# A block of sliding attention and a gated MLP: PSUM tiles with one reader each, another order of the rest products, and another order in three slots

## The chip, the core and the metric

The kernel runs on one core of one Trainium2 chip. The metric is the device time of one execution in microseconds. The engines named below are TensorE (PE, with its weight loads PEld), VectorE (DVE), ScalarE (ACT), GpSimd (POOL) and SyncE (SP); SP and POOL mostly issue transfers. TensorE writes its results to PSUM, and VectorE or ScalarE copy them from there to SBUF.

## The reference

Two branches share a layer norm of x (2048 rows, 576 columns). Branch A is attention: 32 query heads over 16 key and value heads, the last 512 positions of the caches, no mask. Branch B is a gated MLP. The result is x + A * silu(B).

```python
def _A_ref(x, k_cache, v_cache, wq, wo):
    q = (x @ wq).reshape(B, Sq, Hq, Dh).transpose(0, 2, 1, 3)
    k = repeat(k_cache[:, :, Sk - W:, :], rep, axis=1)      # W = 512, rep = 2
    v = repeat(v_cache[:, :, Sk - W:, :], rep, axis=1)
    p = softmax(einsum("bhqd,bhkd->bhqk", q, k) * Dh ** -0.5)
    o = einsum("bhqk,bhkd->bhqd", p, v)
    return o.transpose(0, 2, 1, 3).reshape(B, Sq, Hq * Dh) @ wo

x = A_x
xn = layernorm(x)
s = _A_ref(xn, A_k_cache, A_v_cache, A_wq, A_wo)
g = silu(_B_ref(xn, B_w1, B_w2, B_w3, B_w4))
return x + s * g
```

## The kernel before

Attention is cut into 4 blocks of 512 query rows with 32 heads each, 128 units that the code counts with `u`. One pass of the loop at line 738 is called a slot here. In slot u TensorE makes the query product of unit u + 1 (`stage_q`), the scores of unit u in two halves (`stage_s`, called `scores(0)` and `scores(1)`), and the value product of unit u - 1 in two halves (`stage_v`, called `values(0)` and `values(2)`). Into some slots further work is laid: the output projection with wo of the block before (`wo_part(0)` to `wo_part(3)`, slots `wo_slots`: 45 to 49, 65 to 69 and 97 to 101) and layer-norm steps (`fill`).

The order on TensorE, SP and POOL is the order in which the code is written. VectorE's and ScalarE's order in the loop is the planner's, with the copies out of PSUM at high priority. In the startup ahead of the loop (lines 691 to 722) the order of all engines is as written.

**The query product.** x has 576 columns: four chunks of 128 and a rest of 64. For the first four heads the rest is padded and multiplied like a chunk (line 539). From head 4 on the rests of four or six heads are made together, in a run (`BURSTS`, 23 runs; 16 of six heads, and 7 of four). The rest products use 64 rows of the array each, and two of them go side by side. They are made in the slot ahead of the run's first head, by `rest_q(u, first)` at line 511: the rest of head u goes into the PSUM bank `psq` that already holds its four main products, that of head u + 1 opens the next `psq` bank, and those of the heads behind go in pairs into a tile of two banks each, borrowed from the scores. `score_bank(1)` (tag sc1) takes the second pair and `score_bank(0)` (tag sc0) the third. A pair is copied to SBUF (`rq`) at once, and `stage_q` adds it later, when it copies that head's main product to `qT` (line 547). For heads without `rq` line 549 copies `psq` to `qT`.

The second pair is copied by ScalarE (line 528). Of the third pair, VectorE copies one half and ScalarE the other (lines 525 and 526). Where a tile is read by two engines, the framework makes the second reader wait for the first.

Each half of the scores takes a tile of two banks, sc0 or sc1; ScalarE's exponential (line 560) empties it. In the wo slots both halves go to sc0 and the output projection takes sc1; it ends in a ScalarE copy (`so`, line 279 or 291). The value product has two banks (tag po), one for each half; VectorE empties them with a reciprocal and a product (lines 583 and 584).

**The order within a slot.** In a slot with a run ahead of it (`late_q`), `scores(0)` comes ahead of `stage_q(u + 1)`, and both halves of the values come ahead of `scores(1)`. Three slots are both of this kind and wo slots: 49, 69 and 101, each the last of its five. There the wo work is the narrow part of the projection, 128 products of 64 columns, in four equal parts (`cuts`, line 741).

**The startup.** x of the first block is transposed by TensorE into two PSUM tiles of two banks each (`x_banks`, line 457): four chunks in the first, the rest chunk in the second, which also takes the transposes of the first two key heads (`k01`). `xT_first` (line 467) copies chunks 0, 1 and 4 with VectorE and chunks 2 and 3 with ScalarE. Then come the query products of heads 0 and 1 (line 717). Later a table load for the exponential and the copies of the keys follow.

Of the kernel before, what the change touches and what calls it, by code (L numbers as in the profile page):

```python
# [8 lines left out]
P = 128  # L9
ACT = mybir.ActivationFunctionType  # L10
# [21 lines left out]
def kernel(  # L32
# [266 lines left out]
    with ExitStack() as actx:  # L299
# [155 lines left out]
            nc.sync.dma_start(out=dstT[:, :, tt * P:(tt + 1) * P], in_=src[:, tt, :], transpose=True)  # L455

        def x_banks():
            four = [ps_sc.tile([P, 4, QB], BF16, name="ps_x", tag=f"sc{i}") for i in range(2)]
            return [four[kc // 4][:, kc % 4, :] for kc in range(NDC)], four[1][:, 2:4, :]

        def tr1_first(pss, tts):
            for tt in tts:
# [45 lines left out]
            cols = slice(u % 4 * Dh, (u % 4 + 1) * Dh)  # L508
            return wq_b[(u // 4) % NWQ][:, kc, cols] if kc < NF else wr_first[:, cols]

        def rest_q(u, first):
            xT = xT_b[u // Hq % 2]
            psq_t[u + 1] = ps_pq.tile([P, QB], FP32, name="psq", tag="pq")
            n = bursts[u]
            pair = [score_bank(i) for i in ((0,) if u - 1 in wo_slots else (1, 0)[0:n // 2 - 1])]
            pss = [first, psq_t[u + 1]] + [p[:, i, :] for p in pair for i in range(2)]
            for i, ps in enumerate(pss):
                half = slice(i % 2 * DR, (i % 2 + 1) * DR)
                nc.tensor.matmul(ps[:, :], lhsT=wr_sb[half, (u + i) % Hq // 2, :], rhs=xT[half, NF, :],  # L519
                                 start=(i > 0), stop=(i != 1), skip_group_check=True)  # L520
            for k, p in enumerate(pair):
                rq = rq_pool.tile([P, 2, QB], FP32, name="rq")
                with tc.high_priority(offset=HP):
                    if k:
                        nc.vector.tensor_copy(out=rq[:, 0, :], in_=p[:, 0, :])
                        nc.scalar.activation(out=rq[:, 1, :], in_=p[:, 1, :], func=ACT.Copy)
                    else:
                        nc.scalar.activation(out=rq[:], in_=p[:], func=ACT.Copy)
                for i in range(2):
                    rq_t[u + 2 + 2 * k + i] = rq[:, i, :]  # L530

        def stage_q(u):
            qb = u // Hq
            plain = u < PLAIN
            pos = 0 if plain else u - first_of[u]
            psq = psq_t.pop(u) if pos == 1 else ps_pq.tile([P, QB], FP32, name="psq", tag="pq")
            n = NDC if plain else NF
            for kc in range(n):
                nc.tensor.matmul(psq[:, :], lhsT=wq_main(u, kc), rhs=xT_b[qb % 2][:, kc, :],  # L539
                                 start=(kc == 0 and pos != 1), stop=(kc == n - 1 and (plain or pos != 0)),  # L540
                                 skip_group_check=True)
            if not plain and pos == 0:
                rest_q(u, psq)
            qT = qT_pool.tile([P, QB], BF16, name="qT")
            with tc.high_priority(offset=HP):
                if pos >= 2:
                    behind["qT"] = nc.vector.tensor_tensor(out=qT[:, :], in0=psq[:, :], in1=rq_t.pop(u), op=ALU.add)  # L547
                else:
                    nc.vector.tensor_copy(out=qT[:, :], in_=psq[:, :])  # L549
            qT_t[u] = qT  # L550
# [186 lines left out]
        with tc.manual_schedule(engines={SP, POOL, PE}):  # L737
            for u in range(0, max(max(fill), max(pe_fill)) + 1):
                atoms = pe_fill.get(u, [])
                n = len(atoms)  # L740
                cuts = [0, n // 4, n // 2, 3 * n // 4, n]
                if u == U:
                    cuts = [0, n // 2, n // 2, 3 * n // 4, n]

                def wo_part(i):
                    for fn in atoms[cuts[i]:cuts[i + 1]]:
                        fn()

                def scores(i):
                    if u < U:  # L750
                        stage_s(u, i)

                def values(t0):
                    if 0 <= u - 1 < U:
                        stage_v(u - 1, t0)

                if u == 1:
                    stage_q(2)
                late_q = u + 1 in bursts
                if late_q:  # L760
                    scores(0)
                    if u in wo_slots:
                        wo_part(0)
                if 1 < u < U - 1:
                    stage_q(u + 1)
                if not late_q:
                    scores(0)
                for fn in fill.get(u, []):
                    fn()
                if not (late_q and u in wo_slots):  # L770
                    wo_part(0)
                values(0)
                wo_part(1)
                if late_q:
                    values(2)
                    wo_part(2)
                    scores(1)
                else:
                    scores(1)
                    wo_part(2)  # L780
                    values(2)
                wo_part(3)
                for fn in turn.get(u, []):
                    fn()
# [648 lines left out]
```

## Time and profile before

| what | value |
| --- | --- |
| median of 3 runs | 820.67 us (820.44 to 821.25) |
| the profiled execution's own time | 820.41 us |
| its span, first to last instruction | 818.9 us |
| granted TensorE clock | 1.000 |
| attention | up to about 470 us |
| first part of the MLP | about 479 to 530 us |
| the two large MLP products | about 530 to 815 us |

A line of the timeline has the start in us, the time until the end of its last instruction in us, the engine, the line of the kernel, the operation, the written tile, the read tiles, the shape, the number of instructions that were merged, and in brackets the idle time of the engine ahead of it with what ended it. A line of the waits names who waited for whom, the total in us, how often, and the longest. In a list of one tile or line, an instruction's durations stand as least, median and greatest in ns, with the first and last start in us.

### The profile page before, as it was taken

How to read it: one execution, taken by the hardware profiler on the slowest of the kernel's cores; microseconds unless marked ns; L12 is line 12 of the kernel's file. 1: busy time of each engine (PE TensorE's matmuls, PEld its weight loads, DVE VectorE, ACT ScalarE, POOL GpSimd, SP SyncE). 2: the span in 40 equal slices, each digit the busy share in tenths (PEclk: the TensorE clock that was granted, in tenths of full speed). 3: DMA queues.
4: the chain of work that ended last, by engine and by line, in shares of the span. 5: the costliest groups of instructions: out<-in, count | busy, mean ns of one | idle time of the engine just before them, and what ended most of it. 6: DMA issues, size and time to landing. Idle time of an engine off the chain costs nothing.

```text
span 818.9 us, 19757 instructions
## 1 busy us (share of the span) xinstructions
PE 805.9 (98%) x8158; PEld 471.3 (58%) x8239; DVE 458.5 (56%) x1395; ACT 412.2 (50%) x519; POOL 95.4 (12%) x162
## 2 busy tenths in 40 slices
PE   8999999999999999999999999999999999999997
PEld 6666565556655666555666556555555555555555
DVE  5879685128832579632676528443246636655413
ACT  6777776237733677822777542033233323334520
POOL 3333210100001000000100311272000000000000
PEclk9999999999999999999999999999999999999999
DMA  7995994109722656410553572399100410330101
GB/s 202 189 174 152 197 195 97 55 1 170 154 60 66 125 105 135 99 46 14 115 113 94 82 96 64 76 321 218 63 2 16 85 51 16 48 88 16 45 15 39
DMA packets 136430, 79.75 MB, mean 97 GB/s; under 512 B 113776, under 2 KB 127376, under 8 KB 136336
## 3 DMA queue, kind: packets, MB, share of 16 engines
q1 hardware_dynamic: 123792, 39.91, 27.7%
q0 software_dynamic: 11296, 37.27, 17.2%
q8 instruction: 65, 1.06, 0.6%
q10 hardware_dynamic: 1248, 1.25, 0.5%
q14 instruction: 29, 0.24, 0.1%
HBM read 45.38 MB, written 6.93 MB: 64 GB/s over the span
## 4 chain that ended last, share of the span: by engine, by line
PE 93%; DVE 4%; ACT 1%; issue 1%; POOL 0%; DVEq 0%; ACTq 0%; POOLq 0%
PE ph L1066 14%; PE po L579 13%; PE sc L557 12%; PE psq L539 12%; PE sc L269 12%; PE pm L1103 11%; PE pm L1281 4%; PE pm L1066 3%; PE pm L823 2%; PE pswo L269 2%; PE pr L1103 2%; PE ph L823 1%; PE pr L269 1%; PE sc L519 1%; PE pm L269 1%
## 5 line engine op out<-in xcount | busy, mean ns | idle before, releaser
L560 ACT ACTIVATE pT<-sc 128x1024 bf16<-128x1024 f32 x256 | 250.2, 1022 | 114.8 <-PE sc L557 106.6
L579 PEld LDWEIGHTS <-pT 128*128 128x128 bf16 x2048 | 133.4, 98 | 57.9 <-issue 6.4
L579 PE MATMUL po<-v_sb,pT 128*128 128x129 bf16 x2048 | 156.0, 220 | 0.7 <-ACT pT L560 0.4
L557 PE MATMUL sc<-qT,kT 128*128 128x512 bf16 x507 | 151.0, 379 | 0.4
L1066 PE MATMUL ph<-xT_b,w_s 64*128 64x512 bf16 x976 | 127.3, 376 | 0.0
L539 PE MATMUL psq<-xT_b,wq_b 128*128 128x512 bf16 x450 | 122.4, 379 | 2.8
L1103 PE MATMUL pm<-w_s,h 64*128 64x512 bf16 x864 | 122.1, 377 | 0.0
L1084 ACT ACTIVATE h<-ph 128x512 bf16<-128x512 f32 x67 | 39.4, 597 | 132.7 <-PE ph L1066 130.5
L269 PE MATMUL sc<-wo_sb,oT 128*128 128x512 bf16 (+1 forms) x756 | 101.8, 284 | 1.6 <-ACT so L279 0.8
L1103 PEld LDWEIGHTS <-h 64*128 64x128 bf16 x1728 | 70.6, 94 | 55.4
L269 PEld LDWEIGHTS <-oT 128*128 128x128 bf16 x1024 | 65.2, 98 | 56.3 <-issue 1.6
L584 DVE TENSOR_TENSOR o<-po,ri_b 128x256 bf16<-128x256 f32 x216 | 91.2, 422 | 6.3 <-DVE ri_b L583 0.3
L583 DVE RECIPROCAL ri_b<-po 128x2 f32<-128x2 f32 x256 | 42.4, 165 | 91.9 <-PE po L579 88.3
L1103 PE MATMUL pr<-w_s,h 64*128 64x64 bf16 x864 | 89.9, 189 | 0.0
L1066 PEld LDWEIGHTS <-w_s 64*128 64x128 bf16 x1152 | 55.8, 94 | 48.6 <-issue 0.6
L1082 DVE COPY hx<-ph 128x512 f32<-128x512 f32 x55 | 38.0, 691 | 60.6 <-PE ph L1066 60.6
L547 DVE TENSOR_TENSOR qT<-psq,rq 128x512 bf16<-128x512 f32 x78 | 53.9, 691 | 32.3 <-PE psq L539 31.7
L539 PEld LDWEIGHTS <-wq_b 128*128 128x128 bf16 x504 | 45.9, 98 | 41.6
L557 PEld LDWEIGHTS <-kT 128*128 128x128 bf16 x512 | 45.2, 98 | 29.7 <-issue 1.3
L549 DVE CAST qT<-psq 128x512 bf16<-128x512 f32 x48 | 33.0, 688 | 41.6 <-PE psq L519 25.9
L347 POOL DMA_DIRECT2D wq_b<-in_A_wq_dram x30 | 22.5, 752 | 279.4 <-PE psq L539 278.6
L1084 ACT ACTIVATE h<-hx 128x512 bf16<-128x512 f32 x55 | 34.6, 630 | 6.0 <-DVE hx L1082 1.7
(177 smaller groups left out, 697.9 us busy)
## 6 DMA issues: line engine op xcount, KB each, us to landing
wq_b<-in_A_wq_dram POOLq DMA_DIRECT2D x30, 512.0 KB, 5.0
wo_sb<-in_A_wo_dram POOLq DMA_DIRECT2D x8, 576.0 KB, 5.5
w_s<-in_B_w_dram POOLq DMA_DIRECT2D x9, 512.0 KB, 6.5
w_s<-in_B_w_dram POOLq DMA_DIRECT2D x10, 288.0 KB, 5.2
w_s<-in_B_w_dram POOLq DMA_DIRECT2D x4, 576.0 KB, 5.9
s_b<-s_dram SPq DMA_DIRECT2D x4, 576.0 KB, 6.6
x_b<-in_A_x_dram SPq DMA_DIRECT2D x4, 576.0 KB, 7.4
out_dram<-o SPq DMA_DIRECT2D x15, 144.0 KB, 1.8
```

The costliest lines, as they stand in the source:

```text
L269: nc.tensor.matmul(ps, lhsT=oT_t[qb * Hq + h][:, tt, :], rhs=wo_sb[:, h, lo:hi], start=(i == 0), stop=(i == Hq - 1))
L539: nc.tensor.matmul(psq[:, :], lhsT=wq_main(u, kc), rhs=xT_b[qb % 2][:, kc, :], start=(kc == 0 and pos != 1), stop=(kc == n - 1 and (plain ...
L547: behind["qT"] = nc.vector.tensor_tensor(out=qT[:, :], in0=psq[:, :], in1=rq_t.pop(u), op=ALU.add)
L557: nc.tensor.matmul(sc[:, j, :], lhsT=kT[:, g, kc * P:(kc + 1) * P], rhs=qT_t[u][:, :], start=True, stop=True)
L560: nc.scalar.activation(out=pT[:], in_=sc[:], func=ACT.Exp, scale=SCALE)
L579: nc.tensor.matmul(po[:, j, :], lhsT=pTs[kc][:, tt * P:(tt + 1) * P], rhs=v_sb[:, g, kc, 0:Dh + 1], start=(kc == 0), stop=(kc == KCH - 1))
L583: nc.vector.reciprocal(out=ri, in_=po[:, :, Dh])
L584: nc.vector.tensor_tensor(out=o[:, t0:t0 + 2, :], in0=po[:, :, 0:Dh], in1=ri.unsqueeze(2).to_broadcast([P, 2, Dh]), op=ALU.mult)
L1066: nc.tensor.matmul(ps[i][:, :], lhsT=lhsT, rhs=xT[half, kc, :], start=first, stop=last, skip_group_check=True)
L1082: nc.vector.tensor_copy(out=src[:, :], in_=ps[i][:, :])
L1084: nc.scalar.activation(out=h3[:, :], in_=src[:, :], func=ACT.Gelu_apprx_tanh)
L1103: nc.tensor.matmul(out, lhsT=h3_t[b, fc][half, tt * P:(tt + 1) * P], rhs=w4_s[fc // WS][half, fc % WS, lo:hi], start=key not in started, s ...
```

## The change

Five edits, all of them in attention and its startup.

1. `x_banks` takes three tiles instead of two. The first holds chunks 0 and 1 and the first two key heads (all read by VectorE), the second chunks 2 and 3 (read by ScalarE), and the third, borrowed from the values' po banks, chunk 4 (read by VectorE).
2. The third rest pair is copied by VectorE in one instruction of 1024 columns.
3. The rest products of a run are made in the order 2, 3, 0, 1, 4, 5.
4. `stage_q` is cut in two: `main_q` makes the four main products, `stage_q` the rest and the copy to `qT`. In slots 49, 69 and 101 `main_q` of the next head comes ahead of `scores(0)`. Everywhere else the order of these steps stays.
5. In the same three slots the wo work is cut otherwise: half of it behind `scores(0)`, none between the halves of the values, and a quarter each on both sides of `scores(1)`.

```diff
         def x_banks():
-            four = [ps_sc.tile([P, 4, QB], BF16, name="ps_x", tag=f"sc{i}") for i in range(2)]
-            return [four[kc // 4][:, kc % 4, :] for kc in range(NDC)], four[1][:, 2:4, :]
+            a, b = (ps_sc.tile([P, 4, QB], BF16, name="ps_x", tag=f"sc{i}") for i in range(2))
+            c = ps_po.tile([P, 2, W], BF16, name="ps_x4", tag="po")
+            return [a[:, 0, :], a[:, 1, :], b[:, 0, :], b[:, 1, :], c[:, 0, :]], a[:, 2:4, :]
...
-        def rest_q(u, first):
+        def rest_q(u):
+            first = psq_t[u]
...
-            for i, ps in enumerate(pss):
+            for i in (2, 3, 0, 1, *range(4, n)):
+                ps = pss[i]
...
                     if k:
-                        nc.vector.tensor_copy(out=rq[:, 0, :], in_=p[:, 0, :])
-                        nc.scalar.activation(out=rq[:, 1, :], in_=p[:, 1, :], func=ACT.Copy)
+                        nc.vector.tensor_copy(out=rq[:], in_=p[:])
...
-        def stage_q(u):
+        def main_q(u):
...
-            if not plain and pos == 0:
-                rest_q(u, psq)
+            psq_t[u] = psq
+
+        def stage_q(u):
+            if u not in psq_t or (u in first_of and first_of[u] == u - 1):
+                main_q(u)
+            pos = 0 if u < PLAIN else u - first_of[u]
+            if u in bursts:
+                rest_q(u)
+            psq = psq_t.pop(u)
...
-                if u == U:
+                if u == U or u + 1 in bursts:
                     cuts = [0, n // 2, n // 2, 3 * n // 4, n]
...
                 if late_q:
+                    if u in wo_slots:
+                        main_q(u + 1)
                     scores(0)
                     if u in wo_slots:
                         wo_part(0)
```

In the changed kernel the order of the instructions on SP and POOL is as before. On VectorE, in a run of six, both reciprocals of the values stand behind the long copy and both products behind them, and some layer-norm steps around a run come a few places earlier or later.

## The prediction

> **What bounds the kernel now.** I read the page first: busy shares, granted clock and the chain that ended last.
>
> ```profile
> span 818.9 us, 19757 instructions
> PE 805.9 (98%) x8158; PEld 471.3 (58%) x8239; DVE 458.5 (56%) x1395; ACT 412.2 (50%) x519; POOL 95.4 (12%) x162
> PEclk9999999999999999999999999999999999999999
> PE 93%; DVE 4%; ACT 1%; issue 1%; POOL 0%; DVEq 0%; ACTq 0%; POOLq 0%
> ```
>
> TensorE is busy for 98% of the span, its clock is granted in every slice, and 93% of the chain is TensorE. The change adds and removes no matmul, so it can only win the gaps between matmuls. The busy share hides most gaps: a row's duration runs past the start of the next matmul. So I read distances between starts in the timeline. A full 128x512 matmul takes 0.216 us from start to start, a 128x129 one of L579 0.0565. Some matmul records are missing, so a jump of exactly one matmul is no gap.
>
> Next the stages behind attention, to see whether time won early can reach the end:
>
> ```profile
> 470.00:530.00 60.00, 59.73 (x796) 35.10 (x797) 33.32 (x108) 13.67 (x26) 9.12 (x21) 1.00 0.40 72
> 530.00:780.00 250.00, 249.95 (x3048) 136.32 (x3047) 124.18 (x361) 96.43 (x163) 22.17 (x33) 1.00 0.32 82
> ```
>
> The first number after each length is TensorE: 0.32 us without matmul in 310. No load is waited for there. The order of work on SP's and POOL's queues is the same before and after, and their loads are issued behind attention's own progress, so they move with it. A microsecond won earlier should be a microsecond at the end.
>
> Then one quiet run of six rest products (slot 15, heads 16 to 21), engine by engine:
>
> ```profile
> 53.84 0.39 PE L519 MATMUL psq<-xT_b,wr_sb 64*128 64x512 bf16 x2
> 54.06 0.60 PE L519 MATMUL sc<-xT_b,wr_sb 64*128 64x512 bf16 x4
> 54.26 0.69 DVE L549 CAST qT<-psq 128x512 bf16<-128x512 f32 x1 [0.98 <-PE psq L519]
> 54.48 1.02 ACT L528 ACTIVATE rq<-sc 128x1024 f32<-128x1024 f32 x1 [0.26 <-PE sc L519]
> 54.60 1.08 PE L579 MATMUL po<-v_sb,pT 128*128 128x129 bf16 x16
> 54.87 0.68 DVE L525 COPY rq<-sc 128x512 f32<-128x512 f32 x1
> 55.47 0.16 DVE L583 RECIPROCAL ri_b<-po 128x2 f32<-128x2 f32 x1
> 55.56 0.59 PE L557 MATMUL sc<-qT,kT 128*128 128x512 bf16 x2
> 55.58 0.60 ACT L526 ACTIVATE rq<-sc 128x512 f32<-128x512 f32 x1
> 55.66 0.42 DVE L584 TENSOR_TENSOR o<-po,ri_b 128x256 bf16<-128x256 f32 x1
> ...
> 56.85 0.59 PE L557 MATMUL sc<-qT,kT 128*128 128x512 bf16 x2
> ...
> 57.28 0.22 PE L579 MATMUL po<-v_sb,pT 128*128 128x129 bf16 x1
> ```
>
> L579's sixteen matmuls should end their starts at 54.60 + 16 x 0.0565 + 0.01 = 55.51, but L557 begins at 55.56: it waits for sc1, which ScalarE's L528 copy frees at 54.48 + 1.02 = 55.50, plus some 0.06 for the signal. The gap is 0.05 us.
>
> **The change part by part.** *Copied pairs first.* The rest matmuls run in pairs 0.22 us apart (53.84, 54.06). With i = 2, 3 ahead, L528 starts 0.42 behind 53.84 instead of behind 54.06: at 54.26, done at 55.28, signalled by 55.34, ahead of 55.51. The 0.05 is gone in the runs of six; there are 16 (the count of L525 below): 0.8 us, or 0.7 with the 0.044 that finer starts give. The runs of four have fewer matmuls to hide the copy:
>
> ```profile
> 87.95 1.08 PE L579 MATMUL po<-v_sb,pT 128*128 128x129 bf16 x16
> 88.06 1.02 ACT L528 ACTIVATE rq<-sc 128x1024 f32<-128x1024 f32 x1 [0.26 <-PE sc L519]
> ...
> 89.14 0.38 PE L557 MATMUL sc<-qT,kT 128*128 128x512 bf16 x1
> ```
>
> L557 could start at 87.95 + 0.904 + 0.01 = 88.86 and starts at 89.14, a gap of 0.28. Moving L528 up by 0.22 leaves 0.06. Four such runs stand outside the wo slots (heads 28, 54, 92, 124): 0.9 us. The price of the order is that psq's own rest product ends 0.22 later, and with it the cast L549 of qT; that qT feeds scores of the next slot (56.85), some 1.9 us behind its present end at 54.95, so it costs nothing; without that cover it would be 0.22 a run.
>
> *Third pair by VectorE alone.* Before, VectorE copies one half and ScalarE the other; ScalarE's half waits for VectorE's because both read one tile:
>
> ```profile
> L525 DVE COPY rq<-sc x16: 678/680/684, 21.3 to 436.7; 128x512 f32<-128x512 f32 x16
> ...
>   DVE rq L525: 3.5, 6
> ```
>
> So in 6 of the 16 runs ScalarE waited for VectorE, 3.5 us in total. These are runs in which layer-norm work stands in VectorE's queue. There the exponential that follows L526 is late, and the second half of the next values waits for it:
>
> ```profile
> 203.54 0.39 PE L519 MATMUL psq<-xT_b,wr_sb 64*128 64x512 bf16 x2
> 205.28 0.68 DVE L525 COPY rq<-sc 128x512 f32<-128x512 f32 x1
> 205.99 0.60 ACT L526 ACTIVATE rq<-sc 128x512 f32<-128x512 f32 x1 [0.78 <-DVE rq L525]
> ...
> 207.07 0.28 PE L579 MATMUL po<-v_sb,pT 128*128 128x129 bf16 x2
> 207.56 0.51 PE L579 MATMUL po<-v_sb,pT 128*128 128x129 bf16 x6 [0.21 <-ACT pT L560]
> ```
>
> ```profile
> PE po L579 <- ACT pT L560: 0.4, 2, 0.2
> ```
>
> ```profile
> 40.41 0.78 PE L579 MATMUL po<-v_sb,pT 128*128 128x129 bf16 x8
> ...
> 119.01 0.79 PE L579 MATMUL po<-v_sb,pT 128*128 128x129 bf16 x8
> 224.16 0.93 PE L579 MATMUL po<-v_sb,pT 128*128 128x129 bf16 x8
> ```
>
> At 207.07 two L579 fill 0.11 but the next starts 0.49 later: 0.38, and the waits list has two of this kind. Eight undisturbed L579 show 0.62 (seven starts and one length, 7 x 0.0565 + 0.22), so three runs lose 0.16 (40.41 to 119.01) and one 0.31. Sum 2 x 0.38 + 3 x 0.16 + 0.31 = 1.55, and with 0.08 ahead of one L557 in the same run 1.6 us. Without L526 the exponential follows the scores directly and all of it goes.
>
> The price is on VectorE. No row shows a 128x1024 fp32 copy there. From below: L584's 256 elements take 0.42 and L549's 512 take 0.69, so 512 more cost 0.54: 1.22. From above: two copies of 0.68, 1.36. I take 1.22, since the two rows are of the same engine and source. In the quiet run the cast starts at 54.06 + 0.42 = 54.48, the copy 0.61 behind it (54.26 to 54.87) at 55.09, and ends at 56.31. The sc0 it frees is wanted at 56.85: 0.5 spare. Behind the copy are queued, by the changed kernel's order, both reciprocals and then both products of L584: reciprocals at about 56.23 and 56.33, the first product at 56.42, done 56.84. Behind it waits the po bank for 57.28: 0.4 spare, 0.25 at the upper price. So ten quiet runs pay nothing. In the six busy runs, were the layer-norm steps to stay where they are, the copy would start 1.74 behind the first rest matmul (203.54 to 205.28) against 1.25 in the quiet case; 0.49 of the 0.4 spare is gone, 0.1 to 0.2 each, at most 1.2 us. In the changed VectorE order one such step has moved behind the products in the heaviest runs, so I take 0.15 us for all six, between 0 and 1.2. Net 1.45.
>
> A rule stands against the row of 3.5 us. In the Trainium skill's page PSUM — Partial Sum Buffer, section PSUM bank collisions raise a hardware error, the order between two engines is needed per bank; the halves of this tile lie in two banks, so by it L526 would not wait at all. The trace disagrees (3.5 us in 6 waits). By the page this part would be worth nothing and the sum about 3.1 us.
>
> *The three slots with the new order* (49, 69, 101):
>
> ```profile
> 175.39 0.59 PE L557 MATMUL sc<-qT,kT 128*128 128x512 bf16 x2
> 175.59 0.60 ACT L279 ACTIVATE so<-sc 128x512 bf16<-128x512 f32 x1 [2.82 <-PE sc L269]
> ...
> 176.24 0.83 PE L269 MATMUL sc<-wo_sb,oT 128*128 128x64 bf16 x23 [0.25 <-ACT so L279]
> ```
>
> ```profile
> PE sc L269 <- ACT so L279: 0.8, 3, 0.3
> ```
>
> The first narrow wo product waits for ScalarE to empty the same bank: 176.24 - 175.39 = 0.85 where two matmuls need 0.43, so 0.42, three times. Four main products of 0.216 put ahead cover 0.86: 1.25 us won. What is late next: the rest pair in sc0 needs the exponential of the scores. The scores take 0.59, the signal some 0.1 and the exponential 1.02 (as L528), 1.7 in all; the scores' second half and 64 narrow products at 0.029 give 2.07. No new wait.
>
> *Transposes of x in three tiles:*
>
> ```profile
> 8.80 1.09 DVE L472 COPY xT_b<-ps_x 128x512 bf16<-128x512 bf16 x3 [0.83 <-PE ps_x L464]
> ...
> 9.64 1.08 ACT L470 ACTIVATE xT_b<-ps_x 128x512 bf16<-128x512 bf16 x2 [1.45 <-DVE xT_b L472]
> 9.67 1.49 PE L717 MATMUL psq<-xT_b,wq_b 128*128 128x512 bf16 x4 [0.21 <-DMA wq_b<-in_A_wq_dram]
> ...
> 10.99 0.38 PE L717 MATMUL psq<-xT_b,wo_sb 128*128 128x512 bf16 x1
> ```
>
> ScalarE's two copies wait for VectorE's; they can start at 8.80 and end at 9.88, ahead of need. L717 starts at 9.67 because of a load, so only the gap behind it is won: six matmuls from 9.67 would bring L717's last piece to 9.67 + 5 x 0.216 = 10.75 instead of 10.99: 0.24, with 0 as the other end should that piece's own load be late.
>
> **Sum.** 0.75 + 0.9 + 1.45 + 1.25 + 0.2 = 4.55 us. The profiled execution took 820.41 (span 818.9 and 1.5 around it), so 815.9; the median of the runs is 0.26 above it: 816.1. Bounds: 5.0 us if VectorE costs nothing, 3.3 at its upper price.
>
> **The rivals.** *VectorE is overfull in busy runs.* Its queue keeps the layer-norm work ahead of the long copy: 1.2 instead of 0.15 is paid, 817.2. For it: 0.78 of waiting at 205.99; against it: the moved step.
>
> The Trainium skill's Perfetto Trace Analysis, section Optimizing Scalar/DVE Operations, speaks against merging: where an unsaturated engine causes bubbles, smaller instructions may finish sooner. *One copy frees sc0 later than two halves.* Before it is free at 55.58 + 0.60 = 56.18, after at 56.31: 0.13 later. If scores waited at once, ten quiet runs lose 1.3: 817.4. Against it, they come only at 56.85. The page's rule holds for the release; the trace shows no one who waits.
>
> *The exponentials stay late,* because VectorE's queue and not L526 is the cause: 1.45 is not won, 817.6.
>
> *The gain is swallowed behind attention* by a load or transpose with its own pace: no change, 820.6. It would need 4.5 us of new idle time where 0.32 stands now.
>
> *Slower: the po banks.* The two-bank copy is dear, and the products of L584 behind it hold po in all 16 runs. That decides from a copy of 1.22 + 0.35 = 1.57 us and eats the whole gain at 0.28 more, 1.85. At three times the 512 copy, 2.04, each run loses 0.47, 7.5 us, against 4.4 won: 823.7. Nothing in the rows of VectorE points to such a price, but none shows the form.
>
> **How the numbers follow.** Forecast 0.76; overfull VectorE 0.06, later sc0 0.04, late exponentials 0.05; swallowed 0.05; slower 0.04. The first four are faster by over 0.2% (1.6 us, about what a measurement can tell from no change): 0.91. Same 0.05, slower 0.04. The range 815.2 to 817.8 takes in both bounds and the three milder rivals.
>
> **What would show it.** In the profile after: L557 behind the values with no gap in runs of six and 0.06 in runs of four; ScalarE without a wait for VectorE in its rq copies; eight L579 at 0.62 in the slots behind busy runs; no wait for the so copy; L717's last piece for head 0 near 10.75. I am wrong if VectorE's 1024 copy is over 1.5 us, if L579 or L557 waits for VectorE in the slot behind a run, or if TensorE is idle for microseconds behind 465.

## The result and the profile after

| what | before | after |
| --- | --- | --- |
| median of the runs compared | 820.96 us (820.44 to 822.53, 6 runs) | 815.81 us (815.44 to 816.26, 6 runs) |
| the profiled execution's own time | 820.41 us | 815.91 us |
| its span | 818.9 us | 814.2 us |
| the last matmul starts, from the span's start | 814.02 us | 809.62 us |

The ratio of after to before is 0.9936, with an interval of 0.9923 to 0.9949. A second set of runs of the changed kernel gave 815.64 us (815.18 to 815.81) against 820.48 (820.24 to 821.45), ratio 0.9939 (0.9926 to 0.9953). The forecast was 816.1 us, between 815.2 and 817.8. The medians differ by 5.15 us, with 4.2 to 6.3 by the interval, and by 4.84 in the second set; the profiled executions by 4.50. The forecast gain was 4.55 us.

The page of the changed kernel first: its span, its busy shares, and the chain that ended last.

```profile
span 814.2 us, 19724 instructions
PE 803.1 (99%) x8158; PEld 471.8 (58%) x8239; DVE 462.6 (57%) x1395; ACT 403.4 (50%) x503; POOL 95.5 (12%) x162
PE 98%; DMA 1%; issue 1%; SPq 0%; DVE 0%; ACT 0%
```

TensorE's share of the chain went from 93% to 98%, and VectorE's 4% are gone. ScalarE has 16 instructions and 8.8 us of busy time less, VectorE 4.1 us more. The list of the waits of TensorE's matmuls (who waited for whom, us in total, times, longest) holds three lines; its weight loads have a list of their own, which is used further down.

```profile
PE warm L706 <- POOL ident masks.py:199: 1.9, 1, 1.9
PE psq L726 <- DMA wq_b<-in_A_wq_dram: 0.4, 1, 0.4
PE pm L269 <- issue: 0.2, 1, 0.2
```

All three were there before; the two that stand against the so copy and the exponential have gone.

Short gaps do not show in such lists, so the time won is followed by a **lead**: the start of the same matmul in the profile of before minus its start in the profile of after. The 2048 matmuls of the values (16 per unit) are all recorded in both, and serve as marks. Between the last mark of one unit and that of the next the lead grows only where the change wins something. It is 0.13 us at the first values, 4.41 at the first MLP product (479.05 against 474.65) and 4.40 at the last matmul, so nothing won in attention is lost behind it. By slots:

| where | how often | lead won, us |
| --- | --- | --- |
| startup, up to the first values | 1 | 0.13 |
| slot behind a run of six, VectorE quiet | 10 | 0.04 to 0.05 each, 0.42 |
| slot behind a run of six, VectorE busy (9, 21, 37, 57, 63, 85) | 6 | 0.21, 0.21, 0.21, 0.46, 0.31, 0.38, in all 1.78 |
| slot behind a run of four outside the wo slots | 4 | 0.22 each, 0.86 |
| wo slots 48, 68, 100 by this count | 3 | 0.41 each, 1.24 |

(The runs are numbered by the slot in which their rest products are made. A unit's values are made one slot later, so the slots 49, 69 and 101 stand here as 48, 68 and 100.) The other 0.28 us of the 4.68 that the span lost lie behind the last matmul. In the eleven profiles of changed kernels in this study that stretch was between 0.24 us longer and 0.56 us shorter than before's, so no part of the change is credited with it.

In the timeline, the quiet run that the prediction showed (slot 15):

```profile
53.45 0.39 PE L522 MATMUL sc<-xT_b,wr_sb 64*128 64x512 bf16 x2
53.68 0.38 PE L522 MATMUL psq<-xT_b,wr_sb 64*128 64x512 bf16 x2
53.88 1.02 ACT L530 ACTIVATE rq<-sc 128x1024 f32<-128x1024 f32 x1
54.09 0.69 DVE L558 CAST qT<-psq 128x512 bf16<-128x512 f32 x1 [1.20 <-PE psq L522]
54.22 1.08 PE L588 MATMUL po<-v_sb,pT 128*128 128x129 bf16 x16
54.70 1.21 DVE L528 COPY rq<-sc 128x1024 f32<-128x1024 f32 x1
55.13 0.59 PE L566 MATMUL sc<-qT,kT 128*128 128x512 bf16 x2
55.82 1.02 ACT L569 ACTIVATE pT<-sc 128x1024 bf16<-128x1024 f32 x1 [0.92 <-PE sc L566]
56.03 0.76 DVE L593 TENSOR_TENSOR o<-po,ri_b 128x256 bf16<-128x256 f32 x2
56.43 0.59 PE L566 MATMUL sc<-qT,kT 128*128 128x512 bf16 x2
56.86 0.62 PE L588 MATMUL po<-v_sb,pT 128*128 128x129 bf16 x8
```

ScalarE's copy starts 0.43 us behind the first rest product and ends at 54.90, and the scores follow sixteen values without a gap: 54.22 + 16 x 0.0565 = 55.12. VectorE's long copy ends at 55.91; the sc0 that it frees is wanted at 56.43, 0.5 us later. ScalarE now waits 0.92 us for scores, where before it still had a copy to make. The bracket at the exponential is good news here: ScalarE used to be late here and is early now.

The run of four and the new order in slot 49, from the same view:

```profile
87.22 1.02 ACT L530 ACTIVATE rq<-sc 128x1024 f32<-128x1024 f32 x1
87.33 1.08 PE L588 MATMUL po<-v_sb,pT 128*128 128x129 bf16 x16
88.30 0.59 PE L566 MATMUL sc<-qT,kT 128*128 128x512 bf16 x2
...
174.26 1.03 PE L541 MATMUL psq<-xT_b,wq_b 128*128 128x512 bf16 x4
174.46 0.60 ACT L279 ACTIVATE so<-sc 128x512 bf16<-128x512 f32 x1 [2.82 <-PE sc L269]
175.12 0.59 PE L566 MATMUL sc<-qT,kT 128*128 128x512 bf16 x2
175.55 2.03 PE L269 MATMUL sc<-wo_sb,oT 128*128 128x64 bf16 x64
175.81 1.02 ACT L569 ACTIVATE pT<-sc 128x1024 bf16<-128x1024 f32 x1 [0.76 <-PE sc L566]
177.51 0.39 PE L522 MATMUL sc<-xT_b,wr_sb 64*128 64x512 bf16 x2
```

In the run of four the scores start 88.30 - 87.33 = 0.97 behind the values, of which the sixteen take 0.904 and some 0.01 the change of form: a gap of 0.06, where 0.28 stood. In slot 49 the so copy is done at 175.06, under the four main products and the scores, and the narrow products follow the scores after 0.43, the time of two matmuls. The exponential is done at 176.83, and the rest product that needs its bank comes at 177.51.

### The profile page after: what moved, and what is told of

Same layout as the page of the kernel before. It is cut to its first block, busy times and chain, and to the rows that moved or that the text cites. A ratio compares the mean times of both kernels' runs of the same rounds, so it can differ in the third digit from the quotient of the medians.

```text
span 814.2 us, 19724 instructions
## 1 busy us (share of the span) xinstructions
PE 803.1 (99%) x8158; PEld 471.8 (58%) x8239; DVE 462.6 (57%) x1395; ACT 403.4 (50%) x503; POOL 95.5 (12%) x162
## 3 DMA queue, kind: packets, MB, share of 16 engines
q10 hardware_dynamic: 1248, 1.25, 0.4%
## 4 chain that ended last, share of the span: by engine, by line
PE 98%; DMA 1%; issue 1%; SPq 0%; DVE 0%; ACT 0%
PE po L588 15%; PE ph L1077 15%; PE sc L566 13%; PE psq L541 13%; PE sc L269 12%; PE pm L1114 11%; PE pm L1292 4%; PE pm L1077 3%; PE pm L834 2%; PE pswo L269 2%; PE pr L1114 2%; PE ph L834 1%; PE sc L522 1%; PE pr L269 1%; PE pm L269 1%; DMA wq_b<-in_A_wq_dram 1%
## 5 line engine op out<-in xcount | busy, mean ns | idle before, releaser
L588 PEld LDWEIGHTS <-pT 128*128 128x128 bf16 x2048 | 133.0, 98 | 56.8 <-issue 6.6
L588 PE MATMUL po<-v_sb,pT 128*128 128x129 bf16 x2048 | 154.5, 220 | 0.1
L593 DVE TENSOR_TENSOR o<-po,ri_b 128x256 bf16<-128x256 f32 x216 | 89.9, 421 | 5.3
L592 DVE RECIPROCAL ri_b<-po 128x2 f32<-128x2 f32 x256 | 40.6, 164 | 87.2 <-PE po L588 84.1
L809 DVE TENSOR_SCALAR hx<-ph,ph 1x1 f32<-1x1 f32 x55 | 11.6, 210 | 46.2 <-PE ph L1077 46.2
```

Source lines behind the costliest of these rows:

```text
L588: nc.tensor.matmul(po[:, j, :], lhsT=pTs[kc][:, tt * P:(tt + 1) * P], rhs=v_sb[:, g, kc, 0:Dh + 1], start=(kc == 0), stop=(kc == KCH - 1))
L592: nc.vector.reciprocal(out=ri, in_=po[:, :, Dh])
L593: nc.vector.tensor_tensor(out=o[:, t0:t0 + 2, :], in0=po[:, :, 0:Dh], in1=ri.unsqueeze(2).to_broadcast([P, 2, Dh]), op=ALU.mult)
```

## The experiments

Four kernels make one part of the change alone, in the kernel before, four alter the copy of the third pair in the changed kernel, and two repeat the changed kernel and the best of these. Each result has the median of its runs with the lowest and highest, and the lead in attention (from the first values to the first MLP product), which is read from one profile and is much finer than the medians.

**The three transpose tiles alone.** The edit in the kernel before:

```diff
-            four = [ps_sc.tile([P, 4, QB], BF16, name="ps_x", tag=f"sc{i}") for i in range(2)]
-            return [four[kc // 4][:, kc % 4, :] for kc in range(NDC)], four[1][:, 2:4, :]
+            a, b = (ps_sc.tile([P, 4, QB], BF16, name="ps_x", tag=f"sc{i}") for i in range(2))
+            c = ps_po.tile([P, 2, W], BF16, name="ps_x4", tag="po")
+            return [a[:, 0, :], a[:, 1, :], b[:, 0, :], b[:, 1, :], c[:, 0, :]], a[:, 2:4, :]
```

> The kernel before with the three transpose tiles alone. If ScalarE's copies only waited for VectorE's because of the shared tile, ScalarE starts within 0.15 us of VectorE's first copy and TensorE is ahead of before by 0.1 to 0.25 us at its first MLP product, all of it won ahead of 13 us. If the first load of wq sets the pace, nothing is won (0.0 us).

Measured: 820.35 us (820.05 to 821.96) against 820.53, ratio 1.0 (0.999 to 1.0009). ScalarE's first copy starts 0.12 us behind VectorE's (8.99 and 9.11 in this kernel's timeline), and the last piece of the first head comes 1.09 us behind the first product (9.56 and 10.65), so the gap of 0.23 is gone, as expected. The lead was 0.34 us at the first values, but only 0.06 at the first MLP product, less than the 0.1 to 0.25 that were expected. It shrank by 0.28 in one later slot, where scores waited for an exponential at 340.9, which the profile of before doesn't have. What follows: the part won about as much at the first values as the start itself varies (last section), and by the times it can't be told from nothing. Why the exponential was late in that one slot stays open.

**The order 2, 3, 0, 1 alone,** with the split copy kept:

```diff
-            for i, ps in enumerate(pss):
+            for i in (2, 3, 0, 1, *range(4, n)):
+                ps = pss[i]
```

> The kernel before with the rest products in the order 2, 3, 0, 1, 4, 5 alone, the third pair still split. If the parts of the change add up, TensorE is ahead by 1.5 us (16 runs of 0.04 and four of 0.21). My theory is that they do not: the cast of qT and so VectorE's half copy come later, ScalarE's half waits for it longer, and the busy runs lose 0.1 to 0.2 us more than before, so only 0.5 to 0.9 us are won, 0.86 of it in the four runs of four.

Measured: 820.01 us (819.62 to 820.65), ratio 0.9992 (0.9983 to 1.0002); lead in attention 0.65 us. The four runs of four won 0.22 each, as in the whole change. The quiet runs of six won 0.02 each instead of 0.04, and in the busy ones 9, 21, 37 and 63 0.12 to 0.13 was lost each (57 won 0.13, 85 nothing). ScalarE's waits and TensorE's, in this kernel's lists:

```profile
ACT rq L527 <- DVE rq L526: 10.3, 16, 1.0
```

```profile
PE po L580 <- ACT pT L561: 1.1, 6, 0.2
```

Before, ScalarE waited for VectorE 6 times, 3.5 us in all. Now it is 16 times and 10.3 us, since with the new order psq's own rest product, VectorE's cast and the copy queued behind it all come 0.22 us later, while ScalarE is free earlier. A busy run shows where it ends:

```profile
38.30 0.68 DVE L526 COPY rq<-sc 128x512 f32<-128x512 f32 x1
...
39.01 0.60 ACT L527 ACTIVATE rq<-sc 128x512 f32<-128x512 f32 x1 [0.83 <-DVE rq L526]
...
39.51 1.02 ACT L561 ACTIVATE pT<-sc 128x1024 bf16<-128x1024 f32 x1
...
40.58 0.51 PE L580 MATMUL po<-v_sb,pT 128*128 128x129 bf16 x6 [0.17 <-ACT pT L561]
```

The exponential ends at 40.53, and the next value product starts behind it. By subtraction the order is worth 1.4 us in the whole change (4.28, less 1.65 and 1.23 for the two parts below). It is worth that only where ScalarE doesn't wait for VectorE. One engine for the copy is one way to that and not the only one: with a split copy in which ScalarE's half comes first (below), the order wins its 0.04 us in every quiet run and its 0.22 in every run of four too.

**The copy by VectorE alone,** with the old order:

```diff
-                        nc.vector.tensor_copy(out=rq[:, 0, :], in_=p[:, 0, :])
-                        nc.scalar.activation(out=rq[:, 1, :], in_=p[:, 1, :], func=ACT.Copy)
+                        nc.vector.tensor_copy(out=rq[:], in_=p[:])
```

> The kernel before with the third pair copied by VectorE alone. Theory: the six waits of TensorE for late exponentials go (1.6 us), the 0.05 us ahead of the scores in 16 runs and the 0.28 in four stay; TensorE is ahead by 1.4 to 1.6 us. Rival, VectorE overfull: under 0.6 us, with TensorE waiting for po or sc0 behind the runs.

Measured: 818.77 us (818.08 to 819.64), ratio 0.9978 (0.9968 to 0.9988); lead in attention 1.65 us, all of it in the six busy runs (0.17, 0.17, 0.17, 0.47, 0.31, 0.37) and nothing elsewhere. So the gain of this part is the six waits of ScalarE (3.5 us in sum), as far as they reached TensorE, and the ten quiet runs neither win nor pay.

**The new order in the three slots alone,** with `main_q` made a step of its own as in the whole change:

```diff
+                    if u in wo_slots:
+                        main_q(u + 1)
                     scores(0)
...
-                if u == U:
+                if u == U or u + 1 in bursts:
```

> The kernel before with the new order in the three slots alone. Theory: 0.41 us at each of three places, 1.24 us in all, nothing elsewhere. Rival, the wait goes to the rest pair behind the narrow wo products: 0.3 us or less.

Measured: 819.32 us (819.12 to 819.8), ratio 0.9984 (0.9974 to 0.9994); the lead grew by 0.413, 0.415 and 0.413 in the three slots and by 1.23 over all of attention, and no other place changed by more than 0.015. The wait for the so copy (0.8 us, 3 times) is gone from the matmuls' list.

The next four kernels start from the changed kernel and alter how the third pair is copied, to see why one engine is better than two.

**ScalarE's half first in the code,** split as before:

```diff
-                        nc.vector.tensor_copy(out=rq[:], in_=p[:])
+                        nc.scalar.activation(out=rq[:, 1, :], in_=p[:, 1, :], func=ACT.Copy)
+                        nc.vector.tensor_copy(out=rq[:, 0, :], in_=p[:, 0, :])
```

> The kernel after, with the third pair split again, but ScalarE's half first in the code. If the wait is between two readers of one tile, VectorE now waits for ScalarE in all 16 runs of six, until about 2.0 us behind the first rest product, ScalarE never waits, and TensorE stays within 0.2 us of the kernel after. If only readers of one PSUM bank are kept apart, neither waits for the other, since the halves lie in two banks.

Measured: 815.94 us (815.24 to 816.42), ratio 0.9941 (0.9924 to 0.9957); lead in attention 3.97 us, 0.31 less than the changed kernel's 4.28 (the slots 9, 37 and 57 lost 0.09, 0.04 and 0.28, two others won 0.04 and 0.05). That is more than the 0.2 us of the expectation. Now VectorE is the one that waits. The list of the tile rq, the matmuls' list of waits, and the quiet run of slot 15 in the timeline:

```profile
  ACT rq L528: 3.8, 10
...
  DVE rq L529: 3.8, 10
```

```profile
PE sc L567 <- DVE rq L529: 0.2, 1, 0.2
```

```profile
54.92 0.59 ACT L528 ACTIVATE rq<-sc 128x512 f32<-128x512 f32 x1
...
55.55 0.69 DVE L529 COPY rq<-sc 128x512 f32<-128x512 f32 x1 [0.38 <-ACT rq L528]
```

VectorE starts 0.04 behind ScalarE's end at 55.51, though its half lies in the other bank of the tile. The second reader in the code waits for the first, whichever engine it is. The waits were expected in all 16 runs and came in 10: in the six busy ones VectorE was late by itself, with its half 1.98 to 2.58 us behind the first rest product and no idle time ahead of it. The latest of these, in slot 57, is the one for which scores waited. So a split tile costs little where the engine that has the exponentials to make reads first. The Trainium skill's page PSUM — Partial Sum Buffer, section PSUM bank collisions raise a hardware error, asks for an order between two engines where they touch the same bank. Here two engines that read different banks of one tile are ordered all the same (3.5 us in 6 waits before, 3.8 us in 10 here), so the bank does not decide. The two halves share two tiles, the PSUM tile that they read and the SBUF tile rq that they write, and no run here parts these two. The startup does so for another pair: there both engines write xT_b before and after, and ScalarE's wait went (0.84 us behind VectorE's start, then 0.11) when the PSUM tiles were parted. So the order comes, as far as the runs show, from the PSUM tile, which the framework follows as a whole.

**ScalarE copies the third pair alone,** in one instruction:

```diff
-                        nc.vector.tensor_copy(out=rq[:], in_=p[:])
+                        nc.scalar.activation(out=rq[:], in_=p[:], func=ACT.Copy)
```

> The kernel after, with the third pair copied by ScalarE alone (1.02 us where VectorE took 1.21). Theory: what hurt was ScalarE's wait for VectorE, not its load. Both copies run one after the other and end 2.4 us behind the first rest product, when the scores are ready, so TensorE stays within 0.2 us of the kernel after. Rival, ScalarE's load: 1.02 us more than after per run makes the exponentials late again, 1.5 us or more are lost, with TensorE waiting for pT in runs of six.

Measured: 815.37 us (815.15 to 816.03), ratio 0.9939 (0.9923 to 0.9956); lead in attention 4.41 us, 0.13 above the changed kernel. The difference lies in the slots 57 (0.51 instead of 0.46), 63 (0.35 for 0.31) and 85 (0.43 for 0.38). The copy takes ScalarE 1.02 us. The same busy run in the timelines, first of this kernel and then of the changed one, with the first rest product, the copy, the exponential and the products that free the values' banks:

```profile
201.22 0.39 PE L522 MATMUL sc<-xT_b,wr_sb 64*128 64x512 bf16 x2
...
202.58 1.02 ACT L528 ACTIVATE rq<-sc 128x1024 f32<-128x1024 f32 x1
...
203.60 1.02 ACT L569 ACTIVATE pT<-sc 128x1024 bf16<-128x1024 f32 x1
...
204.63 0.62 PE L588 MATMUL po<-v_sb,pT 128*128 128x129 bf16 x8
```

```profile
201.78 0.39 PE L522 MATMUL sc<-xT_b,wr_sb 64*128 64x512 bf16 x2
...
203.39 1.21 DVE L528 COPY rq<-sc 128x1024 f32<-128x1024 f32 x1
...
204.15 1.02 ACT L569 ACTIVATE pT<-sc 128x1024 bf16<-128x1024 f32 x1 [0.92 <-PE sc L566]
...
204.72 0.76 DVE L593 TENSOR_TENSOR o<-po,ri_b 128x256 bf16<-128x256 f32 x2
...
205.20 0.46 PEld L588 LDWEIGHTS <-pT 128*128 128x128 bf16 x8 [0.34 <-DVE o L593]
205.20 0.63 PE L588 MATMUL po<-v_sb,pT 128*128 128x129 bf16 x8
```

The exponential starts 2.38 us behind the first rest product in the one and 2.37 in the other. ScalarE's longer load costs nothing: what delayed the exponential before was its wait for VectorE and not its work. With VectorE's copy the values start 3.42 us behind it, with ScalarE's 3.41. In the slots 63 and 85, read in the same way, it is 3.44 and 3.45 with VectorE's copy and 3.41 with ScalarE's, while the scores ahead of them start at 2.97 or 2.98 in all of these. The bracket at the weight load names what the values wait for: VectorE's product L593, which empties a po bank and is queued behind the long copy. In the list of the weight loads' waits the products that write o stand 6 times with 1.8 us in the changed kernel and not at all in this one. Most of that is hidden; the 0.13 us are what VectorE's long copy still costs TensorE in busy runs, and they are paid at the po banks.

**A second copy of half the pair on VectorE,** which only repeats work, 0.69 us more behind the long copy:

```diff
                         nc.vector.tensor_copy(out=rq[:], in_=p[:])
+                        nc.vector.tensor_copy(out=rq[:, 0, :], in_=p[:, 0, :])
```

> The kernel after, with 512 columns of the third pair copied a second time by VectorE (0.6 us more in its queue, 16 times). The prediction gave 0.4 to 0.5 us of spare time behind the long copy in quiet runs and about 0.1 in busy ones. So TensorE should lose 0.2 to 0.3 us in each of ten quiet runs and 0.5 to 0.65 in each of six busy ones, 5 to 7 us in all, waiting for sc0 or po; the kernel would be about as slow as before. If there is more room than I think: under 2 us lost.

Measured: 822.54 us (821.85 to 823.44), ratio 1.0026 (1.0017 to 1.0036); 6.5 us of lead lost against the changed kernel, 0.28 or 0.29 in each quiet run but that of slot 15 (0.36 there) and 0.53 to 0.63 in each busy one, as expected. Who waited for the copies, in the list of the tile rq (us, times), and slot 15 in the timeline:

```profile
  PEld L567: 9.2, 13
  PE sc L567: 2.9, 7
```

```profile
56.28 0.69 DVE L529 COPY rq<-sc 128x512 f32<-128x512 f32 x1
56.89 0.41 DVE L594 TENSOR_TENSOR o<-po,ri_b 128x256 bf16<-128x256 f32 x1
57.12 0.59 PE L567 MATMUL sc<-qT,kT 128*128 128x512 bf16 x2 [0.20 <-DVE rq L529]
```

TensorE's matmuls waited 7 times and its weight loads 13 times, all at the scores. The scores start 57.12 - 53.79 = 3.33 behind the first rest product, against 56.43 - 53.45 = 2.98 in the changed kernel. They wait for sc0 until the second copy is done at 56.97. The values follow the scores by 0.43 or 0.44 us in all 16 runs, as they do without a wait, so here the po banks cost nothing more. With 0.69 us added, 0.28 are lost in a quiet run and about 0.6 in a busy one: the cover of the long copy is some 0.4 us in the one and 0.1 in the other. In this kernel the scores are held first, since the second copy keeps sc0 and stands ahead of VectorE's products.

**The long copy in two halves on VectorE:**

```diff
-                        nc.vector.tensor_copy(out=rq[:], in_=p[:])
+                        for i in range(2):
+                            nc.vector.tensor_copy(out=rq[:, i, :], in_=p[:, i, :])
```

> The kernel after, with VectorE's long copy cut into two of 512 columns. Theory: sc0 comes free about 0.07 us later (1.28 instead of 1.21 us), inside the spare time: TensorE within 0.1 us of the kernel after in quiet runs, at most 0.07 lost in each of six busy ones. Rival, smaller pieces finish sooner and help: over 0.3 us faster.

Measured: 816.32 us (815.85 to 816.77), ratio 0.9946 (0.993 to 0.9963); lead in attention 4.11 us, 0.17 less than with one copy, lost in the slots 57, 63 and 85 (0.05 to 0.07 each). Two copies take 1.36 us and one 1.21; of the 0.15 between them a third to a half is paid in three of the busy runs, and nothing elsewhere. It is paid at the po banks again: the scores behind these runs start at 2.97 or 2.98 us as before, and the values at 3.49 to 3.52 instead of 3.42 to 3.45. The Trainium skill's Perfetto Trace Analysis, section Optimizing Scalar/DVE Operations, says smaller instructions may let work finish sooner where an engine that isn't full causes bubbles. No run here shows a gain from it: in the quiet runs nobody waits for the tile, and in the busy ones the extra time counted.

**Both once more, side by side,** the changed kernel and the one in which ScalarE copies both pairs:

> The changed kernel once more, unaltered, beside the version in which ScalarE copies both pairs (next run), so that the two are compared on one chip. The lead of TensorE over the kernel before, by the start of the value products, was 4.28 us within attention in its first profile and 0.13 at the first values. Theory (the lead is fixed by what each slot of attention does and repeats): 4.2 to 4.35 us within attention again, a time near 815.8. Rival (part of the lead was the luck of one execution, as the 0.8 us were that three of the kernels lost in the MLP at one place): a lead that differs by over 0.2 us within attention.

> The changed kernel with the third pair copied by ScalarE alone, once more. Theory (in a busy run the rest of the third pair is late because VectorE still has its own earlier work; ScalarE has none there): a lead within attention of 4.35 to 4.45 us, 0.1 to 0.15 above that of the changed kernel, all of it in the slots 57, 63 and 85; a median 0.1 to 0.2 us below that of the changed kernel on this chip, which the spread of the runs (some 0.8 us) will hardly separate. Rival (the first result was luck): a lead equal to that of the changed kernel within 0.03 us.

Measured: the changed kernel 815.64 us (815.18 to 815.81), lead in attention 4.28; with ScalarE alone 815.48 us (815.39 to 815.86), lead 4.43. The slots 57, 63 and 85 have 0.46, 0.31 and 0.38 again against 0.51, 0.35 and 0.43. The lead by slots repeats within about 0.01 us between executions. By the medians the two can't be told apart, as their runs overlap; by the lead the kernel with ScalarE alone is ahead both times, by 0.13 us in these three slots. By the lead it is the best version of the study; its ratio to the kernel before is 0.9940 (0.9926 to 0.9953).

## Why the prediction was right, step by step

The forecast was 4.55 us won, and the lead at the last matmul is 4.40. Four of the five terms came out a little smaller than forecast and one a little larger, each by at most 0.1, so the agreement of the sum is not made by errors that cancel. In a busy run the lead can't be divided between the order and the copy; the table takes there the order's 0.041 of the quiet runs.

| step | forecast | by the lead |
| --- | --- | --- |
| order of the rest products, runs of six | 0.75 | 0.66 (16 at the quiet runs' 0.041) |
| order, runs of four | 0.9 | 0.86 |
| third pair by VectorE alone, net | 1.45 | 1.53 (1.78 less 6 x 0.041); 1.65 with the old order |
| three slots | 1.25 | 1.24 |
| startup | 0.2 | 0.13; 0.29 in the second profile |

**Copied pairs first.** Right in place and size, with gaps of none and 0.06 us as foretold. One thing was not said: this order alone makes the split copy worse, as the experiment with the order alone showed. The prediction priced the 0.22 us by which the cast of qT comes later at nothing because its scores are far off, and did not name there the copy that is queued behind the cast. For the one long copy it did count from the later cast, in its working of the third pair (55.09), and in quiet runs that copy ends with 0.5 us to spare, so the omission cost the forecast nothing.

**Third pair.** The list of the tile rq in the profile after has the copy, with its least, median and greatest duration in ns:

```profile
L528 DVE COPY rq<-sc x16: 1210/1214/1215, 21.4 to 432.8; 128x1024 f32<-128x1024 f32 x16
```

The copy takes 1.214 us, where 1.22 was worked out from two shorter rows, and 1.57 was the point from which the po banks were to decide. The spare for sc0 is 0.5, as forecast. The price in busy runs was taken as 0.15 us, at the po banks behind the long copy; ScalarE alone, which does not pay it, gained 0.13 more in both of its profiles, at these banks. So one sign that the prediction named for being wrong did come, in a size that it had priced: behind busy runs L588's weight loads wait for VectorE. The matmuls' list of waits doesn't show it. In the profile after, the layer-norm step that the changed order had moved stands behind both products (their row at 204.72; the step at 205.39), and the copy started 203.39 - 201.78 = 1.61 behind the first rest product, not 1.74. That the waiting and not ScalarE's load made the exponentials late is shown by the kernel with ScalarE alone: more load, no wait, the same start of the exponential.

**The three slots.** 0.413 to 0.415 each against 0.42, alone and together; no new wait.

**Startup.** The two engines' copies and the first head's products, from the timeline after:

```profile
8.60 1.08 DVE L473 COPY xT_b<-ps_x 128x512 bf16<-128x512 bf16 x3 [0.75 <-PE ps_x L465]
8.71 1.09 ACT L471 ACTIVATE xT_b<-ps_x 128x512 bf16<-128x512 bf16 x2 [0.63 <-PE ps_x L465]
...
9.78 1.25 PE L726 MATMUL psq<-xT_b,wq_b 128*128 128x512 bf16 x4 [0.39 <-DMA wq_b<-in_A_wq_dram]
...
10.87 0.38 PE L726 MATMUL psq<-xT_b,wo_sb 128*128 128x512 bf16 x1
```

ScalarE starts 0.11 us behind VectorE instead of 0.84. From L726's start to its last piece it is 10.87 - 9.78 = 1.09, five matmuls without a gap, where it was 1.32: the 0.23 are won. But the load of wq landed 0.11 later in this execution, so the piece came at 10.87 and not at 10.75.

**The rivals.** Overfull VectorE at its price of 1.2 us, late exponentials and later sc0 are ruled out by the slots behind busy and quiet runs. That the gain is swallowed behind attention is ruled out by the leads at the MLP (4.41) and at the end (4.40). The po banks as the slower outcome would have needed a copy of 1.57 us. The kernel with the second copy, 0.69 us more on VectorE, shows that too much copying on VectorE does eat the gain (6.5 us lost); there sc0 is what TensorE waits for. With one long copy it is the po banks, as the rival said, in three busy runs and for 0.13 us. The rival's price at 2.04 us of copying, 7.5 us, is of the size that 1.21 + 0.69 = 1.90 us of copying cost, but a single copy of that length was not tried.

**What the forecast did not see.** Its upper bound of 5.0 us is more than its own terms give without a price on VectorE: 0.8 + 0.9 + 1.6 + 1.25 + 0.24 = 4.8. It also held that behind attention no load is waited for. That is so in the profiles of before and after, but not in every execution, as the last section shows.

## What to carry to other kernels

In this framework, give each PSUM tile one reader, even where two engines would read different banks of it and each half is shorter: the second reader starts when the first is done, and inherits all the work that the first has queued ahead. Where a tile must have two readers, let the engine on which the next work hangs read first: here that came within 0.31 us of one reader. Price such a merge by the slot behind it, with who needs the tile and who is queued behind the copy, in quiet and in busy stretches apart. Where the expected gain is within the scatter of the runs, follow one matmul's start through both traces: by slots it repeated within about 0.01 us here, where medians of five runs could not separate 0.13. Read the waits of the weight loads beside those of the matmuls.

## What the runs showed beside this

**A transfer with little spare behind attention.** In three of the profiled executions (the order alone, the copy alone, the two halves) TensorE lost 0.8 to 0.93 us at one place in the MLP. The timeline of the kernel with the copy alone:

```profile
488.34 1.28 DVE L897 COPY hs<-hq 32x512 bf16<-32x512 bf16 x4 [1.27 <-DMA hq<-h]
...
490.24 1.04 PE L822 MATMUL pm<-xT_b,hb 64*128 64x512 bf16 x8 [0.56 <-DVE fence L797]
```

VectorE waits for a transpose of h, and TensorE for VectorE. In the changed kernel the same copy starts without a wait:

```profile
484.05 1.27 DVE L909 COPY hs<-hq 32x512 bf16<-32x512 bf16 x4
```

That is 9.4 us behind the first MLP product (474.65), against 10.7 to 10.9 in the three. These three executions took 0.45 to 0.61 us more than the medians of their kernels (819.38 against 818.77 for the copy alone), which fits a delay that most executions don't have; only profiled ones could be looked into. What delays the transpose was not tried.

**The start of a kernel varies.** The first values came between 0.19 us later and 0.69 earlier than in the profile of before. The eight profiles with the changed startup spread from 0.11 to 0.69 (mean 0.37), and the three others with the old one from -0.19 to 0.21, though the code up to there is the same within each group. A gain of 0.2 us there can be read from one gap, not from the time.

**A change of shape on TensorE costs 0.1 us.** In each run the first 64-row product starts 0.31 us behind the start of the last 128-row one, where 0.216 is usual, and the first value product starts 0.31 or 0.32 behind the last 64-row one: 0.1 us each time, before and after. (In the changed kernel's three slots the 64-row products follow narrow ones of 64 columns, at 0.126 instead of 0.029: 0.1 again.) At 23 runs these are some 4.5 us, and in attention no other regular gap of that size is left. The Trainium skill's page TensorEngine Tiling (Array Packing), section Key Properties, says that changing the tiling mode drains TensorE, which fits; no run here tried to take it away.
